# Reordered loads, two chunks of attention first, and out-stages held back until w3 @ w_out is there, in a retention-plus-FFN kernel on one core

## The chip, the core and the metric

The kernel runs on one core of one Trainium2 chip. The metric is the device time of one execution in microseconds. Times in the profile are microseconds from the first instruction, unless marked ns. PE is TensorE's matmuls, PEld its weight loads, DVE VectorE, ACT ScalarE, POOL GpSimd, SP the engine that issues the DMAs.

## The reference

q, k and v have 4 sequences, 8 heads, 768 positions and 64 values per head. A recurrent retention with a decay per head makes y, which is laid out as 3072 tokens of 512 values, and a multiplicative FFN follows:

```python
gamma = 1.0 - 2.0 ** (-5.0 - np.arange(H))
for t in range(S):
    state = gamma * state + einsum('bhd,bhe->bhde', k[:, :, t], v[:, :, t])
    y[:, :, t] = scale * einsum('bhd,bhde->bhe', q[:, :, t], state)
x = y.transpose(0, 2, 1, 3).reshape(B * S, H * D)      # 3072 x 512
h = ((x @ w1) * (x @ w2)) @ w3                         # w1, w2: 512 x 1024; w3: 1024 x 1024
out = h @ w_out                                        # w_out: 1024 x 512
```

## The kernel before

**Attention.** The tokens are cut into 24 chunks of 128, six to a sequence. For chunk n, `casts(n)` (line 181) makes fp16 copies of q on ScalarE and k on GpSimd, and GpSimd multiplies v by the decay table VS into one of three zero-padded buffers VP. `transposes(n)` (204) turns q and k on TensorE and evicts them: kT and qT on VectorE, the zero-padded QP in two halves on ScalarE. `scores(n)` (222) makes the masked score matrix `am`, `kv(n)` (240) the state for the next chunk (`s` on VectorE, `t` on GpSimd, tables GS), and `outputs(n)` (262) sums am against VP and the state against qT, and writes the chunk's part of XT with the table YS (271).

**FFN.** `ffn_tile` (276) takes a tile of 256 or 512 tokens. An A unit is four matmuls of a w1 column block against XT, evicted to `pa` by ScalarE; a B unit the same with w2, multiplied with pa by VectorE into `ht` (296). An out-stage (302) multiplies eight ht blocks by W3O = w3 @ w_out and writes 128 rows of the output. W3O is computed once: `w3_transpose` (151) and `w3_mm` (161), eight times each.

**Order of the work.** The schedule is manual: each engine runs its instructions in the order in which the program writes them, and waits where a semaphore says so. All DMAs are issued by SP, in program order too. The program writes: tables and zeroing (81 to 119), loads and casts of w_out and w3 (130 to 146) and the w3 product (171 to 175), then loads of chunks 0 and 1, loads and casts of w1 and w2 (360 to 368), more chunks, and the loop over 24 steps (373). Step n issues casts(n + 2), transposes(n + 1), scores(n), kv(n) and outputs(n), with FFN units pulled in between, spread evenly over the steps until the next tile is complete:

```python
m = -(-a // left)
parts = [m // 4 + (1 if i < m % 4 else 0) for i in range(4)]
```

The tiles are two of 256 tokens and five of 512; an out-stage of a tile follows each second pair of units of the next tile. Weights pass through six stage buffers (`wstage`), chunk loads through six buffers each for q, k and v, PSUM results of the FFN through three banks (`psF`).

Of the kernel before, what the change touches and what calls it, by code (L numbers as in the profile page):

```python
# [9 lines left out]
FP = mybir.dt.float32  # L10
HP = mybir.dt.float16
AF = mybir.ActivationFunctionType
MULT = mybir.AluOpType.mult
# [5 lines left out]
def kernel(  # L19
# [11 lines left out]
    nc = tc.nc  # L31
# [27 lines left out]
    def stage(w_ap, i, ncol):  # L59
        t = wstage.tile([128, ncol], FP, tag="wst", name="stg")  # L60
        nc.sync.dma_start(t[:, :], w_ap[i * 128 : (i + 1) * 128, :])
        return t
# [3 lines left out]
    def load_chunk(n):  # L66
        if n >= NSTEP:
            return
        b, c = divmod(n, NCH)
        tiles = []  # L70
        for nm, src in (("q", q), ("k", k), ("v", v)):
            t = ld.tile([128, 512], FP, tag=nm + "32", name=nm + "32")
            nc.sync.dma_start(
                t[:, :].rearrange("p (h d) -> p h d", d=D),
                src[b, :, c * C : (c + 1) * C, :].rearrange("h i d -> i h d"),
            )
            tiles.append(t)
        chunk_in[n] = tiles


    ident = const.tile([128, 128], FP, name="ident")
    make_identity(nc, ident[:, :])
    ident16 = const.tile([128, 128], HP, name="ident16")
    nc.vector.tensor_copy(ident16[:, :], ident[:, :])

# [5 lines left out]
    ip_f = const.tile([128, H], FP, name="ip_f")  # L91
    nc.vector.tensor_copy(ip_f[:, :], ip_i[:, :])
    if_f = const.tile([128, 128], FP, name="if_f")
    nc.vector.tensor_copy(if_f[:, :], if_i[:, :])


    VS = const.tile([128, H], FP, name="VS")
    YS = const.tile([128, NP, 128], FP, name="YS")
    GS = const.tile([128, NP, 128], FP, name="GS")
    nc.vector.memset(GS[:, :, :], 0.0)  # L100
    for h in range(H):
        lg = math.log(gam[h])
        p, r = h // 2, (h % 2) * 64
        nc.scalar.activation(VS[:, h : h + 1], ip_f[:, h : h + 1], AF.Exp, scale=-lg)
        nc.scalar.activation(YS[r : r + 64, p, :], if_f[r : r + 64, :], AF.Exp, scale=lg)
        nc.vector.memset(GS[r : r + 64, p, r : r + 64], gam[h] ** C)

    keep = const.tile([128, 128], FP, name="keep")
    nc.vector.memset(keep[:, :], 1.0)
# [6 lines left out]
    QP = [const.tile([128, NP, 2, 128], HP, name=f"qp{i}") for i in range(2)]  # L116
    VP = [const.tile([128, NP, 2, 128], HP, name=f"vp{i}") for i in range(3)]
    for t in QP + VP:
        nc.gpsimd.memset(t[:, :, :, :], 0.0)
# [4 lines left out]
    W1 = [wpool.tile([128, DFF], HP, name=f"w1_{i}") for i in range(4)]  # L124
    W2 = [wpool.tile([128, DFF], HP, name=f"w2_{i}") for i in range(4)]
    WO = [wpool.tile([128, DM], HP, name=f"wo_{i}") for i in range(8)]
    W3 = [wpool.tile([128, DFF], HP, name=f"w3_{i}") for i in range(8)]
    W3O = [wpool.tile([128, DM], HP, name=f"w3o_{i}") for i in range(8)]

    wo_st = [stage(moe_w_out, i, DM) for i in range(2)]  # L130
    w3_st = [stage(moe_w3, 0, DFF)]
    wo_st += [stage(moe_w_out, i, DM) for i in range(2, 4)]
    nc.scalar.copy(WO[0][:, :], wo_st[0][:, :])
    nc.scalar.copy(WO[1][:, :], wo_st[1][:, :])
    nc.vector.tensor_copy(W3[0][:, :], w3_st[0][:, :])  # L135
    nc.scalar.copy(WO[2][:, :], wo_st[2][:, :])
    nc.scalar.copy(WO[3][:, :], wo_st[3][:, :])
    for i in range(4, 8):
        t = stage(moe_w_out, i, DM)
        nc.scalar.copy(WO[i][:, :], t[:, :])  # L140
    for i in range(1, 8):
        t = stage(moe_w3, i, DFF)
        if i % 2 == 0:
            nc.vector.tensor_copy(W3[i][:, :], t[:, :])
        else:
            nc.scalar.copy(W3[i][:, :], t[:, :])


    w3t = {}

    def w3_transpose(f):
        ps = ps_t.tile([128, 1024], HP, tag="psT", name="psT")
        for g in range(8):
            nc.tensor.transpose(  # L154
                ps[:, g * 128 : (g + 1) * 128], W3[f][:, g * 128 : (g + 1) * 128], ident16[:, :]
            )
        t = att.tile([128, 1024], HP, tag="w3t", name="w3t")
        nc.vector.tensor_copy(t[:, :], ps[:, :])  # L158
        w3t[f] = t

    def w3_mm(f):
        t = w3t.pop(f)
        ps = ps_f.tile([128, DM], FP, tag="psF", name="psW")
        for g in range(8):
            nc.tensor.matmul(  # L165
                ps[:, :], lhsT=t[:, g * 128 : (g + 1) * 128], rhs=WO[g][:, :],
                start=(g == 0), stop=(g == 7),
            )
# [12 lines left out]
    def casts(n):  # L181
# [80 lines left out]
    def outputs(n):  # L262
# [10 lines left out]
        )  # L273


    def ffn_tile(tok0, TB):
        hts = []

        def unit(f):
            psA = ps_f.tile([128, TB], FP, tag="psF", name="psFA")  # L280
            for d in range(4):
                nc.tensor.matmul(  # L282
                    psA[:, :], lhsT=W1[d][:, f * 128 : (f + 1) * 128], rhs=XT[:, d, tok0 : tok0 + TB],
                    start=(d == 0), stop=(d == 3),
                )
            pa = fsb.tile([128, TB], FP, tag="pa", name="pa")
            nc.scalar.copy(pa[:, :], psA[:, :])  # L287
            yield
            psB = ps_f.tile([128, TB], FP, tag="psF", name="psFB")
            for d in range(4):  # L290
                nc.tensor.matmul(  # L291
                    psB[:, :], lhsT=W2[d][:, f * 128 : (f + 1) * 128], rhs=XT[:, d, tok0 : tok0 + TB],
                    start=(d == 0), stop=(d == 3),
                )
            ht = fsb.tile([128, TB], HP, tag=f"ht{f}", name=f"ht{f}")
            nc.vector.tensor_tensor(ht[:, :], pa[:, :], psB[:, :], MULT)  # L296
            hts.append(ht)
            yield

        def out_unit(tb):  # L300
            psO = ps_f.tile([128, DM], FP, tag="psF", name="psO")
            for f in range(8):
                nc.tensor.matmul(  # L303
                    psO[:, :], lhsT=hts[f][:, tb * 128 : (tb + 1) * 128], rhs=W3O[f][:, :],
# [4 lines left out]
            r0 = tok0 + tb * 128  # L309
            nc.sync.dma_start(out[r0 : r0 + 128, :], osb[:, :])  # L310

        return unit, out_unit, TB // 128

    tiles = [(0, 256), (256, 256)] + [(512 * i, 512) for i in range(1, 6)]

    def ffn_all():

        pending = []
        for tok0, TB in tiles:
            unit, out_unit, nout = ffn_tile(tok0, TB)  # L320
            for f in range(8):
                for _ in unit(f):
                    yield tok0 + TB
                if pending and f % 2 == 1:
                    fn, tb = pending.pop(0)
                    fn(tb)
                    yield tok0 + TB
            pending += [(out_unit, tb) for tb in range(nout)]
        while pending:
            fn, tb = pending.pop(0)  # L330
            fn(tb)
            yield 0

    need = []
    for i, (tok0, TB) in enumerate(tiles):
        nprev = tiles[i - 1][1] // 128 if i else 0
        need += [tok0 + TB] * (16 + nprev)
    need += [0] * 4
    gen = ffn_all()
    done = [0]  # L340

    def avail(ntok):

        m = done[0]
        while m < len(need) and need[m] <= ntok:
            m += 1
        return m - done[0]

    def pull(m):
        for _ in range(m):  # L350
            if done[0] < len(need):
                next(gen)
                done[0] += 1


    PRE = 5
    for n in range(2):
        load_chunk(n)
    w_st = []
    for nm, w_ap, dst in (("1", moe_w1, W1), ("2", moe_w2, W2)):  # L360
        for i in range(4):
            t = stage(w_ap, i, DFF)
            if i % 2 == 0:
                nc.vector.tensor_copy(dst[i][:, :], t[:, :])
            else:
                nc.scalar.copy(dst[i][:, :], t[:, :])
        if nm == "1":
            casts(0)
    for n in range(2, PRE):
        load_chunk(n)  # L370
    transposes(0)
    casts(1)
    for n in range(NSTEP):
        load_chunk(n + PRE)
        ready = n * C
        a = avail(ready)

        left = max(1, next((t0 + tb for t0, tb in tiles if t0 + tb > ready), NTOK) // C - n)
        m = -(-a // left)
        parts = [m // 4 + (1 if i < m % 4 else 0) for i in range(4)]  # L380
        casts(n + 2)
        transposes(n + 1)
        pull(parts[0])
        scores(n)
        pull(parts[1])
        t_new = kv(n)
        pull(parts[2])
        outputs(n)
        Tst[0] = t_new
        pull(parts[3])  # L390
    pull(len(need))
# [30 lines left out]
```

## Time and profile before

| | |
|---|---|
| median of 3 runs | 235.93 us (235.54 to 236.34) |
| profiled execution | 236.38 us |
| its span, first to last instruction | 234.7 us |
| TensorE matmuls busy | 194.7 us, 83% of the span |
| VectorE, ScalarE, GpSimd busy | 120.0, 105.5, 67.7 us |
| mean granted TensorE clock | 0.978 of full |
| DMA | 35.9 MB, mean 153 GB/s |

The profile has the busy time of each engine, 40 slices of the span, the chain of work that ended last followed back from the end, and groups of instructions by line with the mean time of one and what ended the idle time before them. Matmuls are pipelined, so the mean duration of one is longer than the distance between two. The profiled execution lies 0.45 us above the median of the runs.

### The profile page before, as it was taken

To read this page: it belongs to the slowest core of one execution; us is meant where nothing else is said; L and a number is where in the kernel's file an instruction comes from. 1 tells how busy PE (TensorE), PEld (TensorE's weight loads), DVE (VectorE), ACT (ScalarE), POOL (GpSimd) and SP (SyncE) were. 2 spreads that over 40 slices of the span, in tenths; PEclk is the share of its full clock that TensorE was granted. 3 is DMA by queue.
4 is the path that set the end of the run, shared out by engine and by line. 5 is a ranking of instruction groups with operands and counts; after the bars stand their busy time and mean duration, and the time that the engine had idled before them with its cause. 6 is when DMAs were issued, how large, how long until landed. Compare 5 with 4: busy or idle time off the path is not lost.

```text
span 234.7 us, 3859 instructions
## 1 busy us (share of the span) xinstructions
PE 194.7 (83%) x1408; PEld 116.2 (49%) x1408; DVE 120.0 (51%) x225; ACT 105.5 (45%) x193; POOL 67.7 (29%) x102
## 2 busy tenths in 40 slices
PE   0100899458988798999999999999999999999993
PEld 0100455237875585556655555555555555544441
DVE  3403224349776568667765576654666556432300
ACT  8443222774553454356435433554434542334332
POOL 4500330035545343424720553242332322000000
PEclk9999999857999999999999999999999999999999
DMA  5599994899997769586955566865601111011123
GB/s 196 196 355 375 210 376 172 254 213 219 211 216 148 170 142 188 129 182 146 218 84 144 118 124 157 179 144 123 136 1 47 45 45 47 27 64 45 47 89 135
DMA packets 81811, 35.91 MB, mean 153 GB/s; under 512 B 75648, under 2 KB 75648, under 8 KB 81792
## 3 DMA queue, kind: packets, MB, share of 16 engines
q1 hardware_dynamic: 81792, 35.66, 61.1%
q8 instruction: 11, 0.18, 0.4%
q14 instruction: 8, 0.07, 0.1%
HBM read 29.36 MB, written 6.29 MB: 152 GB/s over the span
## 4 chain that ended last, share of the span: by engine, by line
PE 63%; DVE 14%; ACT 8%; DMA 7%; issue 5%; SPq 1%; DVEq 0%; ACTq 0%
PE psO L303 18%; PE psFA L282 14%; PE psFB L291 10%; DVE am L232 8%; PE psW L165 7%; DMA stg<-in_moe_w_dram 5%; ACT qp L219 3%; PE psY L267 3%; ACT pa L287 2%; PE psA L229 2%; PE psT L210 2%; PE psT L212 2%; DMA stg<-in_moe_w_out_dram 2%; DVE ht L296 2%; PE psT L154 2%
## 5 line engine op out<-in xcount | busy, mean ns | idle before, releaser
L296 DVE TENSOR_TENSOR ht<-pa,psFB 128x512 f16<-128x512 f32 (+1 forms) x56 | 34.0, 607 | 51.6 <-ACT pa L287 33.3
L291 PE MATMUL psFB<-xt,w 128*128 128x512 f16 (+1 forms) x224 | 50.7, 349 | 2.6 <-ACT pa L287 2.5
L282 PE MATMUL psFA<-xt,w 128*128 128x512 f16 (+1 forms) x224 | 50.7, 349 | 0.9 <-DVE xt L271 0.9
L303 PE MATMUL psO<-w3o,ht 128*128 128x512 f16 x192 | 44.7, 380 | 0.0
L308 ACT ACTIVATE osb<-psO 128x512 f32<-128x512 f32 x24 | 14.3, 597 | 64.1 <-PE psO L303 64.1
L259 POOL TENSOR_TENSOR t<-s,GS 128x512 f16<-128x512 f32 x16 | 20.4, 1272 | 65.6 <-DVE s L258 57.1
L287 ACT COPY pa<-psFA 128x512 f32<-128x512 f32 (+1 forms) x56 | 28.8, 525 | 19.1 <-PE psFA L282 18.6
L196 POOL TENSOR_TENSOR vp<-v,VS 128x256 f16<-128x256 f32 x48 | 28.5, 615 | 13.6 <-PE psY L270 8.6
L232 DVE TENSOR_TENSOR am<-psA,keep 128x512 f16<-128x512 f32 x48 | 30.8, 682 | 0.4 <-PE psA L229 0.3
L291 PEld LDWEIGHTS <-w 128*128 128x128 f16 x224 | 21.3, 98 | 19.2 <-issue 3.3
L188 POOL CAST k<-k 128x512 f16<-128x512 f32 x24 | 14.6, 610 | 46.8 <-DMA k<-in_k_dram 36.7
L282 PEld LDWEIGHTS <-w 128*128 128x128 f16 x224 | 20.7, 98 | 13.8 <-DVE xt L271 0.8
L303 PEld LDWEIGHTS <-ht 128*128 128x128 f16 x192 | 18.1, 98 | 18.9
L154 PE MATMUL psT<-ident,w 128*128 128x128 f16 x64 | 5.7, 242 | 23.2 <-DVE w3t L158 13.7
L218 ACT COPY qp<-psT 64x512 f16<-64x512 f16 x24 | 13.9, 578 | 17.0 <-DVE qT L217 7.1
L267 PE MATMUL psY<-am,vp 128*128 128x128 f16 x96 | 18.0, 221 | 3.9 <-DVE am L232 2.1
L216 DVE COPY kT<-psT 128x512 f16<-128x512 f16 x24 | 10.2, 423 | 20.0 <-PE psT L212 19.9
L268 PE MATMUL psY<-am,vp 128*128 128x128 f16 x96 | 18.1, 223 | 0.0
L154 PEld LDWEIGHTS <-w 128*128 128x128 f16 x64 | 4.9, 109 | 25.0 <-DVE w L135 9.4
L271 DVE TENSOR_TENSOR xt<-psY,YS 128x512 f16<-128x512 f32 x24 | 16.4, 685 | 0.5 <-PE psY L270 0.3
L165 PE MATMUL psW<-wo,w3t 128*128 128x512 f16 x64 | 16.5, 409 | 0.0
L229 PE MATMUL psA<-qp,kT 128*128 128x256 f16 x96 | 15.3, 285 | 0.0
(49 smaller groups left out, 203.3 us busy)
## 6 DMA issues: line engine op xcount, KB each, us to landing
stg<-in_moe_w_dram SPq DMA_DIRECT2D x16, 512.0 KB, 6.7
q<-in_q_dram SPq DMA_DIRECT2D x24, 256.0 KB, 4.8
k<-in_k_dram SPq DMA_DIRECT2D x24, 256.0 KB, 4.9
v<-in_v_dram SPq DMA_DIRECT2D x24, 256.0 KB, 4.8
out_dram<-osb SPq DMA_DIRECT2D x24, 256.0 KB, 2.0
stg<-in_moe_w_out_dram SPq DMA_DIRECT2D x8, 256.0 KB, 3.9
```

The source lines that it names most:

```text
L165: nc.tensor.matmul(ps[:, :], lhsT=t[:, g * 128 : (g + 1) * 128], rhs=WO[g][:, :], start=(g == 0), stop=(g == 7),)
L196: nc.gpsimd.tensor_tensor(vp[:, :, r, r * 64 : r * 64 + 64], v32[:, :].rearrange("j (p s e) -> j p s e", s=2, e=64)[:, :, r, :], VS[:, :]. ...
L229: nc.tensor.matmul(ps[:, i, :, :], lhsT=kT[:, p, :], rhs=qp[:, p, :, :], start=True, stop=True)
L232: nc.vector.tensor_tensor(am[:, half * 2 : half * 2 + 2, :, :].rearrange("j p s i -> j (p s) i"), ps[:, :, :, :].rearrange("j p s i -> j ( ...
L259: nc.gpsimd.tensor_tensor(t16[:, :, :], s32[:, :, :], GS[:, :, :], MULT)
L267: nc.tensor.matmul(ps[:, p, :], lhsT=vp[:, p, 0, :], rhs=am[:, p, 0, :], start=True, stop=False)
L268: nc.tensor.matmul(ps[:, p, :], lhsT=vp[:, p, 1, :], rhs=am[:, p, 1, :], start=False, stop=(c == 0))
L282: nc.tensor.matmul(psA[:, :], lhsT=W1[d][:, f * 128 : (f + 1) * 128], rhs=XT[:, d, tok0 : tok0 + TB], start=(d == 0), stop=(d == 3),)
L287: nc.scalar.copy(pa[:, :], psA[:, :])
L291: nc.tensor.matmul(psB[:, :], lhsT=W2[d][:, f * 128 : (f + 1) * 128], rhs=XT[:, d, tok0 : tok0 + TB], start=(d == 0), stop=(d == 3),)
L296: nc.vector.tensor_tensor(ht[:, :], pa[:, :], psB[:, :], MULT)
L303: nc.tensor.matmul(psO[:, :], lhsT=hts[f][:, tb * 128 : (tb + 1) * 128], rhs=W3O[f][:, :], start=(f == 0), stop=(f == 7),)
```

## The change

**Loads.** SP issues chunks 0 and 1 first, then the left column halves of w1 and w2 (w1 and w2 of a row block side by side in one stage tile), chunks 2 and 3, the right halves, chunks 4 and 5, then w_out (four loads) and w3 (eight), then chunks 6 to 9. The stage buffers are still six, and a w3 tile has four fp16 buffers of its own (`w3h`) in place of eight lasting ones.

**Tables and zeroing.** QP and VP are zeroed by VectorE, as fp32 words; GpSimd writes the logarithms of the decay, and ScalarE makes VS in one exponential and YS in four.

**Order.** Chunks 0 and 1 go through attention before any FFN. Then units f = 0 to 3 of the first tile run between chunks 2 and 3, those of the second tile behind them, units 4 to 7 of both between chunks 4 and 5, and all units of the third tile with the casts of w_out and w3 between them. The w3 product follows, with the start of chunks 6 and 7 in its end. Only then do out-stages come: the six of the first three tiles head the queue from which steps 6 to 23 take their units, by estimated cost instead of by count. The tiles are five of 256 tokens, three of 512 and one of 256.

```diff
+    def load_w12(half):
+        got = []
+        for d in range(4):
+            t = new_stage()
+            for i, w in enumerate((moe_w1, moe_w2)):
+                dma_in(
+                    t[:, i * 512 : (i + 1) * 512],
+                    w[d * 128 : (d + 1) * 128, half * 512 : (half + 1) * 512],
+                )
+            got.append(t)
+        return got
...
+    load_chunk(0)
+    load_chunk(1)
...
+    def zero(t):
+        nc.vector.memset(t[:, :, :, :].rearrange("p a b c -> p (a b c)").bitcast(FP), 0.0)
...
-    for t in QP + VP:
-        nc.gpsimd.memset(t[:, :, :, :], 0.0)
...
+    def pull(self, cost, ntok):
+        self.credit += cost
+        while self.units and self.units[0][0] <= ntok and self.credit >= self.units[0][1] / 2:
+            need, c, fn = self.units.pop(0)
+            fn()
+            self.credit -= c
...
+    w12a = load_w12(0)
+    load_chunk(2)
+    load_chunk(3)
+    w12b = load_w12(1)
+    load_chunk(4)
+    load_chunk(5)
+
+    casts(0)
+    transposes(0)
+    casts(1)
+    scores(0)
+    transposes(1)
...
+    outputs(1, t_new)
+    cast_w12(0, w12a)
+    wo_st = load_wo()
+    w3_st = [load_w3(f) for f in range(8)]
...
+    for i in range(8):
+        fill.run(2)
+        if i < 2:
+            cast_wo(wo_st, i + 2)
+        elif i < 6:
+            cast_w3(w3_st, i - 2)
+    w3_transpose(0)
+    for f in range(8):
+        if f + 4 < 8:
+            cast_w3(w3_st, f + 4)
+        if f + 1 < 8:
+            w3_transpose(f + 1)
+        if f == 5:
+            casts(6)
+        if f == 7:
+            transposes(6)
+            casts(7)
+        w3_mm(f)
+
+    fill.units = f0.o_units() + f1.o_units() + f2.o_units()
```

The order of SP's queue at the start. Before (`stg` is a weight's stage tile; moe_w stands for w1, w2 and w3):

```order
L61 DMA stg<-in_moe_w_out_dram 128x512 x2
L61 DMA stg<-in_moe_w_dram 128x1024
L61 DMA stg<-in_moe_w_out_dram 128x512 x6
L61 DMA stg<-in_moe_w_dram 128x1024 x7
L73 DMA q_392<-in_q_dram 128x8x64
L73 DMA k_394<-in_k_dram 128x8x64
L73 DMA v_396<-in_v_dram 128x8x64
```

The same queue of the changed kernel:

```order
L60 DMA q_87<-in_q_dram 128x8x64
L60 DMA k_89<-in_k_dram 128x8x64
L60 DMA v_91<-in_v_dram 128x8x64
L60 DMA q_93<-in_q_dram 128x8x64
L60 DMA k_95<-in_k_dram 128x8x64
L60 DMA v_97<-in_v_dram 128x8x64
L60 DMA stg<-in_moe_w_dram 128x512 x8
L60 DMA q_189<-in_q_dram 128x8x64
```

Sixteen loads of w_out and w3 stood ahead of the first q; now six chunk loads stand ahead of the first weight, and w_out comes behind chunk 5.

VectorE's queue of the changed kernel, from the second transposed chunk to the first FFN product (`w_0`, `w_2` are fp16 tiles of w1 and w2 side by side, `s` the state before its decay):

```order
L248 COPY kT<-psT 128x512
L249 COPY qT<-psT 128x512
L287 TENSOR_TENSOR t_281<-psK,GS 128x512
L303 TENSOR_TENSOR xt<-psY,YS 128x4x128
L264 TENSOR_TENSOR am<-psA_294,keep 128x512
L264 TENSOR_TENSOR am<-psA_298,keep 128x512
L290 TENSOR_TENSOR s_308<-psK,t_281 128x512
L303 TENSOR_TENSOR xt<-psY,YS 128x4x128
L175 CAST w_0_161<-stg 128x1024
L175 CAST w_2_163<-stg 128x1024
L335 TENSOR_TENSOR ht_353<-pa,psF 128x256
```

The casts of w1 and w2, which stood ahead of all attention, now stand behind the second xt write and ahead of the first product.

ScalarE's queue of the changed kernel around the third tile, from the last units of the second (`wo` and `w3h` are fp16 tiles of w_out and w3):

```order
L331 COPY pa<-psF 128x256 x2
L177 CAST wo_165<-stg 128x1024
L177 CAST wo_166<-stg 128x1024
L331 COPY pa<-psF 128x256 x3
L177 CAST wo_167<-stg 128x1024
L331 COPY pa<-psF 128x256
L177 CAST wo_168<-stg 128x1024
L331 COPY pa<-psF 128x256 x2
L177 CAST w3h<-stg 128x1024
L331 COPY pa<-psF 128x256 x2
L177 CAST w3h<-stg 128x1024
```

The casts of w_out and w3 stood at the head of this queue; now they stand between the evictions of units.

## Rows read from the trace of the kernel before

**Rows 1.** The page: matmul busy time, and TensorE's share in 40 slices, in tenths.

```profile
PE 194.7 (83%) x1408; PEld 116.2 (49%) x1408; DVE 120.0 (51%) x225; ACT 105.5 (45%) x193; POOL 67.7 (29%) x102
...
PE   0100899458988798999999999999999999999993
```

**Rows 2.** The chain that ended last, in order of time: start, us, what.

```profile
15.55 7.29 DMA stg<-in_moe_w_dram
...
24.20 1.01 PE psT L154 x8
25.22 3.26 PE psW L165 x8
28.48 0.45 PE psT L154 x8
28.93 1.73 PE psW L165 x8
...
43.28 0.59 ACT w3o L169
...
45.76 0.53 ACT q L186
...
57.97 0.60 PE psFA L282 x4
58.56 0.44 PE psFB L291 x4
...
99.73 0.86 PE psFA L282 x4
...
122.51 1.73 PE psO L303 x8
...
144.42 1.73 PE psO L303 x8
...
222.44 8.65 PE psO L303 x40
231.15 0.60 ACT osb L308
```

**Rows 3.** Four stretches of time, with busy us of each engine.

```profile
core 0: us, PE busy (x) PEld busy (x) DVE busy (x) ACT busy (x) POOL busy (x), PEclk, DMA share, GB/s
2.00:4.00 2.00, 0.00 (x0) 0.00 (x0) 1.50 (x10) 1.94 (x11) 0.00 (x0) 1.00 0.84 299
16.00:18.00 2.00, 0.00 (x0) 0.11 (x1) 0.33 (x1) 1.04 (x1) 0.00 (x0) 1.00 1.04 424
50.00:55.00 5.00, 4.69 (x35) 3.99 (x36) 3.56 (x7) 2.37 (x5) 2.94 (x5) 0.50 1.14 220
56.00:58.00 2.00, 1.47 (x21) 1.22 (x21) 2.00 (x5) 1.31 (x3) 0.69 (x1) 1.00 1.24 221
```

**Rows 4.** The q loads: time from issue to landing over all 24.

```profile
DMA to landing us min/median/max: 3.3/4.8/7.4
```

**Rows 5.** VectorE's timeline: XT writes of chunks 1, 3 and 7; start, us.

```profile
57.22 0.69 DVE L271 TENSOR_TENSOR xt<-psY,YS 128x512 f16<-128x512 f32 x1
...
69.28 0.68 DVE L271 TENSOR_TENSOR xt<-psY,YS 128x512 f16<-128x512 f32 x1
...
91.55 0.68 DVE L271 TENSOR_TENSOR xt<-psY,YS 128x512 f16<-128x512 f32 x1
```

**Rows 6.** Groups by line and shape: count | busy us, mean ns | idle before.

```profile
L366 ACT CAST w<-stg 128x1024 f16<-128x1024 f32 x4 | 4.0, 1046 | 0.0
L119 POOL MEMSET vp<- 128x1024 f16 x3 | 2.7, 951 | 0.0
L364 DVE CAST w<-stg 128x1024 f16<-128x1024 f32 x4 | 2.6, 688 | 2.2 <-DMA stg<-in_moe_w_dram 2.2
L135 DVE CAST w<-stg 128x1024 f16<-128x1024 f32 x1 | 2.4, 2441 | 2.9 <-DMA stg<-in_moe_w_dram 2.9
```

More of the change, by code (lines that the diff above doesn't have):

```diff
@@ L56, with dma_in @@
     ctx.enter_context(tc.manual_schedule())
[L59 to L62, printed above, removed]
+    def dma_in(dst, src):
+        nc.sync.dma_start(dst, src)
     chunk_in = {}
@@ L113 @@
     )
-    QP = [const.tile([128, NP, 2, 128], HP, name=f"qp{i}") for i in range(2)]
-    VP = [const.tile([128, NP, 2, 128], HP, name=f"vp{i}") for i in range(3)]
-    for t in QP + VP:
-        nc.gpsimd.memset(t[:, :, :, :], 0.0)
+    VS = const.tile([128, H], FP, name="VS")
+    YS = const.tile([128, NP, 128], FP, name="YS")
+    GS = const.tile([128, NP, 128], FP, name="GS")
+    vs_x = const.tile([128, H], FP, name="vs_x")
+    nc.vector.tensor_tensor(vs_x[:, :], ip_i[:, :], LGH[:, :], MULT)
@@ new lines @@
+    if_f = const.tile([128, 128], FP, name="if_f")
+    nc.vector.tensor_copy(if_f[:, :], if_i[:, :])
+    nc.scalar.activation(VS[:, :], vs_x[:, :], AF.Exp)
+    for p in range(NP):
+        nc.scalar.activation(YS[:, p, :], if_f[:, :], AF.Exp, scale=LGP[:, p : p + 1])
+    zero(QP[0])
+    zero(VP[0])
+    zero(QP[1])
+    zero(VP[1])
+    nc.vector.memset(GS[:, :, :], 0.0)
+    for h in range(H):
+        p, r = h // 2, (h % 2) * 64
+        nc.vector.memset(GS[r : r + 64, p, r : r + 64], gam[h] ** C)
@@ L121 @@
+    zero(VP[2])
     XT = xpool.tile([128, NP, NTOK], HP, name="xt")
[L124 to L127, printed above, removed]
+    W12 = [wpool.tile([128, 2, 2, 512], HP, name=f"w12_{i}") for i in range(4)]
+    WO = [wpool.tile([128, 2, DM], HP, name=f"wo_{i}") for i in range(4)]
@@ L128 @@
     W3O = [wpool.tile([128, DM], HP, name=f"w3o_{i}") for i in range(8)]
[L130 to L144, printed above, removed]
-        else:
-            nc.scalar.copy(W3[i][:, :], t[:, :])
-    w3t = {}
+    W3h = {}
+    w3t = {}
+    def cast_to(dst, src, on_dve):
+        if on_dve:
+            nc.vector.tensor_copy(dst, src)
+        else:
+            nc.scalar.copy(dst, src)
+    def cast_w12(half, got):
+        for d in range(4):
+            cast_to(W12[d][:, half, :, :].rearrange("p a n -> p (a n)"), got[d][:, :], d % 2 == 0)
@@ L308, in out_unit @@
             nc.scalar.activation(osb[:, :], psO[:, :], AF.Copy, scale=final_scale)
-            r0 = tok0 + tb * 128
+            r0 = self.tok0 + tb * 128
             nc.sync.dma_start(out[r0 : r0 + 128, :], osb[:, :])
[L312 to L370, printed above, removed]
+        def ab_units(self, fs):
+            cost = self.TB / 512 * 0.87
+            need = self.tok0 + self.TB
+            u = []
+            for f in fs:
+                u.append((need, cost, lambda f=f: self.a_unit(f)))
+                u.append((need, cost, lambda f=f: self.b_unit(f)))
+            return u
@@ new lines, in o_units, with __init__, available, run @@
+        def o_units(self):
+            return [(0, 1.73, lambda tb=tb: self.o_unit(tb)) for tb in range(self.TB // 128)]
+    class Queue:
+        def __init__(self):
+            self.units, self.credit = [], 0.0
+        def available(self, ntok):
+            s = 0.0
+            for need, cost, _ in self.units:
+                if need > ntok:
+                    break
+                s += cost
+            return s
+        def pull(self, cost, ntok):
[4 more added lines that the diff above has]
+                self.credit -= c
+            if not self.units or self.units[0][0] > ntok:
+                self.credit = 0.0
+        def run(self, m=None):
+            for _ in range(len(self.units) if m is None else m):
+                self.units.pop(0)[2]()
@@ new lines, with step @@
+    fill = Queue()
+    def step(n, look=1):
+        ready = n * C
+        nxt = next((t0 + tb for t0, tb in tiles if t0 + tb > ready), NTOK)
+        share = fill.available(ready) / max(1, nxt // C - n)
+        casts(n + 1 + look)
+        transposes(n + 1)
+        fill.pull(share * 0.25, ready)
+        scores(n)
+        fill.pull(share * 0.25, ready)
+        t_new = kv(n)
+        fill.pull(share * 0.25, ready)
+        outputs(n, t_new)
+        fill.pull(share * 0.25, ready)
+    tiles = [(256 * i, 256) for i in range(5)] + [(1280 + 512 * i, 512) for i in range(3)] + [(2816, 256)]
@@ L371 @@
+    w12a = load_w12(0)
[5 more added lines that the diff above has]
+    casts(0)
     transposes(0)
     casts(1)
[L373 to L390, printed above, removed]
@@ L391 @@
-    pull(len(need))
+    scores(0)
+    transposes(1)
+    t_new = kv(0)
+    outputs(0, t_new)
+    scores(1)
+    t_new = kv(1)
+    outputs(1, t_new)
+    cast_w12(0, w12a)
+    wo_st = load_wo()
+    w3_st = [load_w3(f) for f in range(8)]
+    f0 = Ffn(*tiles[0], 4)
+    fill.units = f0.ab_units(range(0, 4))
+    fill.run(2)
+    casts(2)
+    transposes(2)
+    fill.run(2)
+    scores(2)
+    casts(3)
+    fill.run(1)
+    t_new = kv(2)
+    fill.run(1)
+    transposes(3)
+    outputs(2, t_new)
@@ new lines @@
+    fill.run(2)
+    scores(3)
+    t_new = kv(3)
+    outputs(3, t_new)
+    f1 = Ffn(*tiles[1], 4)
+    fill.units = f1.ab_units(range(0, 4))
+    fill.run(4)
+    cast_w12(1, w12b)
+    fill.run(4)
+    fill.units = f0.ab_units(range(4, 8)) + f1.ab_units(range(4, 8))
+    fill.run(2)
+    casts(4)
+    transposes(4)
+    fill.run(2)
+    scores(4)
+    fill.run(2)
+    casts(5)
+    t_new = kv(4)
+    fill.run(2)
+    transposes(5)
+    outputs(4, t_new)
+    fill.run(2)
+    scores(5)
+    fill.run(2)
@@ new lines @@
+    cast_wo(wo_st, 0)
+    cast_wo(wo_st, 1)
+    t_new = kv(5)
+    fill.run(2)
+    outputs(5, t_new)
+    fill.run(2)
+    f2 = Ffn(*tiles[2], 4)
+    fill.units = f2.ab_units(range(8))
+    for n in range(6, 10):
+        load_chunk(n)
+    for i in range(8):
+        fill.run(2)
+        if i < 2:
[14 more added lines that the diff above has]
+        w3_mm(f)
@@ new lines @@
+    fill.units = f0.o_units() + f1.o_units() + f2.o_units()
+    late = []
+    for i, (tok0, TB) in list(enumerate(tiles))[3:]:
+        f = Ffn(tok0, TB, 4 if TB == 256 else 2)
+        for j in range(0, 8, 2):
+            fill.units += f.ab_units((j, j + 1))
+            if late:
+                fill.units.append(late.pop(0))
+        fill.units += late
+        late = f.o_units()
+    fill.units += late
+    for n in range(6, NSTEP):
+        load_chunk(n + 4)
+        step(n)
+    fill.run()
```

109 lines of the change are left out of this document (59 added, 50 removed).

## The prediction

> **What bounds the kernel now.** I read the page's busy times first, then the chain of waits, then stretches of time, and last groups by shape. TensorE is busy 83% of the span, and its slices show where the rest lies: next to nothing in the first four slices of 5.9 us, a dip in the eighth and ninth, and nines from the seventeenth on [rows 1]. So from about 98 us the kernel is bound by TensorE, and what can be won lies ahead of that.
>
> The chain says what fills the start [rows 2]. The weights w_out and w3 come in until 22.8 us, the product w3 @ w_out begins in earnest with the transposes at 24.20 and its last eviction starts at 43.28, and only at 45.76 does the first q chunk get its cast, though attention needs nothing of these weights. The first FFN matmul issues at 57.97. The last out-stage matmul ends at 222.44 + 8.65 = 231.1 us, and 3.6 us of eviction and store follow, up to 234.7.
>
> The clock matters too. Between 50 and 55 us the granted clock is 0.50 with TensorE busy 4.69 of 5 us, and at 56 to 58 it is 1.00 [rows 3]: levels of 1.2 and 2.4 GHz. The chain shows the same levels at the start of w3: the first eight w3 matmuls take 3.26 us, the next eight 1.73.
>
> **Prices.** At the full clock, from rows 2: eight transposes 0.45 us, so 0.056 each; a unit of four 256-column matmuls 0.44, one of 512 columns 0.86; an out-stage or w3 group of eight 1.73. A chunk's attention is 24 matmuls of 128 columns and four of 256: 24 x 0.056 + 0.44 = 1.78 us. A step in the dense part lasts (144.42 - 122.51) / 3 = 7.30 us for four units, one out-stage and one chunk, 6.95 us of work: 0.35 lost per step.
>
> **The change, step by step.**
>
> *Chunk 0 first.* Its q DMA now goes out at about 0.8 us, where the first DMA goes out today. A q load takes 3.3 us to land at the least, 4.8 in the median, 7.4 at most [rows 4], so the cast starts between 4.1 and 8.2 us. I take 5.3, near the median, since the queue is empty then, and because ScalarE has its exponentials to do first (five instead of sixteen). That is 40.5 us before 45.76.
>
> *Two chunks before any FFN.* From that cast to the end of the second xt write takes 57.22 + 0.69 - 45.76 = 12.1 us today [rows 2, 5]. scores(0) now stands ahead of the second transposes, which frees it of one q cast of 0.62; I take 11.6 us, so xt(1) ends at 16.9.
>
> *w1/w2 casts behind it.* VectorE's two casts are queued behind xt(1), so the first unit waits for both: 2 x 0.69 = 1.4 us by the casts of today's w1, w2; ScalarE's two (1.05 each) are done earlier [rows 6]. The one w3 cast made while GpSimd zeroed took 2.44, so the upper bound is 4.9. I take 1.4, because GpSimd's zeroing, beside which the long one ran, is gone, but keep the bound: GpSimd is now making t and the next k at that moment. FFN starts at 16.9 + 1.4 = 18.3; say 18.4.
> The Trainium skill, "SBUF — State Buffer", section "Who interferes with whom", says that a VectorE cast in a two-port mode and a GpSimd instruction exclude each other for a whole instruction. It agrees with 2.44 beside 0.69, and speaks against this placing: by it the pair would end near the upper bound, and the whole some 2 to 3 us later.
>
> *Zeroing.* Five memsets of 0.95 us leave GpSimd [rows 6] for VectorE, which has nothing to do before the first transposes. Both lie beside the wait for chunk 0: nothing. If chunk 0 landed at 4.1 they would show, by under 1 us.
>
> *Work from 18.4 on.* FFN: 48 units of 512 columns, 41.3; 96 of 256, 42.2; 24 out-stages, 41.5. Attention of 22 chunks: 39.2, less 0.22 for each of three first and four last chunks of a sequence, 1.5. The w3 product, moved from the start to behind f2: 8 x (0.45 + 1.73) = 17.4. Together 180.1 us.
>
> *Cold clock.* TensorE does little before 18.4, so I expect 1.2 GHz there and, for a first stretch like that of 50 to 55, the low level still: half of 5 us lost, 2.5. Bounds: 0, and the second rival.
>
> *Idle TensorE from 18.4 on.* Today the stretch from 57.97 to 231.1, 173.1 us, holds 124.4 of FFN and 37.2 of attention, so 11.5 idle. Now:
> - chunks 2 and 3: xt(1) to xt(3) took 12.1 us with 16 units [rows 5]; only eight are ready now (half of w1, w2 is there). Work 3.5 + 3.6 + 2.5 cold = 9.6. The chain from transposes over evictions to xt does not shorten, so I take 12.4: 2.8 idle.
> - chunks 4 and 5: filled as today's chunks 2 and 3, 0.4 each: 0.8.
> - ScalarE's weight casts: two pairs of 1.05 stand in its queue between evictions of units (after the first four f1 units; before kv(5)). TensorE runs three psF banks ahead, about 1.3 us: 0.8 each. Six casts in f2: 0.5. Start of w3: 0.7. Sum 2.8.
> - steps 6 to 23: 18 x 0.35 = 6.3, and 0.6 more in steps 10 to 13, which have only 2.6 us of units each. Steps of that kind took (91.55 - 69.28) / 4 = 5.57 us today for 4.95 of work [rows 5]. Sum 8.7.
>
> Together 15.1. The DMA queue holds no term. In it w_out and w3 wait for stage buffers, thus for casts ScalarE makes at some 43 to 50 us, and chunk 6 waits behind w3. But w3 lands 2 to 3 us after each cast and is needed one every 2.17, and chunk 6 is needed near 67: covered. If the casts slip, the w3 loop is late next.
>
> **Sum.** 18.4 + 180.1 + 2.5 + 15.1 = 216.1 for the last matmul, + 3.6 = 219.7, against the span of 234.7: 15.0 less. The profiled execution took 236.38, 0.45 over the median 235.93. From the median: **220.9 us**.
>
> **Rivals.**
> *Loads late (0.17).* Chunk loads run at 220 GB/s [rows 3]; 4 KB-row weights at 424; the first 2 KB-row weights at 299. I reckoned w1, w2 near 300 to 400. If everything ran at 220, the first half of w1 and w2 (14 loads of 262 KB) would land at about 2 + 16.7 = 18.7 instead of some 16, and chunk 5 (34 loads) at 42.5, where I need it near 36. That makes FFN start 1.5 late and chunk 5 another 4: 226. For it: in 50 to 55 the engines are full at that rate. Against: the weights are 4 of 8.9 MB.
>
> *The clock stays down (0.04), ending slower.* The work from 18.4 to the w3 loop is 48 units and four chunks, 28.2 us at the full clock. If the waits for chunks 2 to 5 kept TensorE at 1.2 GHz throughout, it would cost 28.2 rather than 2.5: 247. It decides from the point where 17.5 us of this work ran at half. For it: 0.50 was held at a busy share of 0.94 from 50 to 55. Against: it rose right after, and then never fell, also in slices with 7 and 8 tenths [rows 1, 3].
>
> *The start overlaps better (0.15).* Cast at 4.1, no cold loss, and idle time as today's 11.5: 220.9 - 1.2 - 2.5 - 3.6 = 213.6.
>
> *The change does nothing for the end (0.02).* If w3 took TensorE's time at its new place and the steps behind were starved, 236. The printed order speaks against it: six tiles' worth of units lie behind it.
>
> **How the numbers follow.** The forecast has 0.62. The range is 213.5 to 228.0: it takes in the good rival, the loads' rival, and the two casts at 4.9 with the late landing of chunk 0. About 2 in 10 lie outside, beyond these ends and in the slow rival. Under and over 0.3% is what a measurement here can tell from no change; all but the second and the last rival are well below it: faster 0.94, same 0.02, slower 0.04.
>
> **What would show it.** First q cast near 5 us; first FFN matmul near 18; xt(3) near 30; the w3 loop from about 55 to 73 without waits longer than 0.3; then steps like today's, with TensorE nines to the end; granted clock 0.5 until 22 to 25 and 1.0 after. Wrong if w1/w2 casts wait for DMA, if the clock falls again in the waits for chunk 3, or if ScalarE's queue starves the w3 loop.

## The result and the profile after

| | before | changed |
|---|---|---|
| median of 4 runs | 235.74 us | 222.94 us (222.27 to 223.81) |
| profiled execution | 236.38 us | 223.81 us |
| its span | 234.7 us | 222.1 us |

The ratio is 0.9465, with a 95% interval of 0.9408 to 0.9521: 12.8 us less by the medians. Ratios are of means, and a run more than 1.5% above the fastest of its kernel is left out of them. The forecast was 220.9, within 213.5 to 228.0, so the time came out 2.0 us over it. Several terms were wrong, and two large errors cancelled.

The page of the changed kernel, the lines of [rows 1] and the granted clock:

```profile
PE 194.0 (87%) x1536; PEld 128.3 (58%) x1536; DVE 125.0 (56%) x244; ACT 104.0 (47%) x194; POOL 65.1 (29%) x114
...
PE   0366769688999989988999999999999999999992
...
PEclk9997976999999999999999999999999999999999
```

TensorE works from the second slice on, but has holes until the tenth, where [rows 1] had almost nothing in four slices and a dip in two. The granted clock dips in the fourth slice and falls again in the sixth and seventh.

The chain that ended last, as in [rows 2] (start, us, what):

```profile
10.87 5.84 DMA q<-in_q_dram
16.75 1.91 DVE w L175 x2
18.70 0.41 PE psF L318 x2
...
31.03 0.70 DVE xt L303
31.78 6.16 PE psF L318 x32
...
49.20 0.96 ACT wo L177
50.16 0.91 issue
51.07 0.38 ACT pa L331
51.48 0.42 DVE ht L335
51.90 0.61 DVE xt L303
...
61.53 0.61 PE psT L196 x8
62.14 1.73 PE psW L207 x8
...
161.48 1.73 PE psO L340 x8
168.44 1.73 PE psO L340 x8
...
212.89 5.20 PE psO L340 x24
218.16 0.60 ACT osb L345
```

The first unit waits for VectorE's weight casts until 18.7. The profile puts a q load ahead of these casts, but they do not read it: in VectorE's queue they stand behind xt(1), which ends at 16.83. XT of chunk 3 is written at 31.03, and the 32 matmuls behind it take 6.16 us where 3.5 are due at the full clock. At 49 a ScalarE cast of w_out stands ahead of an eviction, and through VectorE's product ahead of XT of chunk 5. The w3 product starts at 61.5, some 6 us later than forecast. From 126 us on the chain is TensorE alone, and a step takes 168.44 - 161.48 = 6.96 us: the work itself, 6.95.

Stretches of time, columns as in [rows 3]:

```profile
18.10:31.78 13.68, 9.76 (x89) 7.61 (x89) 8.44 (x17) 4.84 (x10) 5.83 (x8) 0.81 1.09 264
31.78:61.50 29.72, 25.32 (x220) 20.40 (x220) 16.59 (x37) 17.59 (x34) 5.42 (x8) 0.91 0.78 235
61.50:80.70 19.20, 18.14 (x137) 10.30 (x137) 6.78 (x11) 8.90 (x15) 5.39 (x9) 1.00 1.04 213
80.70:126.00 45.30, 42.50 (x407) 32.15 (x405) 31.07 (x64) 24.19 (x49) 18.77 (x27) 1.00 0.84 172
126.00:180.00 54.00, 54.00 (x405) 31.61 (x403) 37.04 (x65) 27.32 (x48) 21.02 (x30) 1.00 0.56 120
...
30.00:36.00 6.00, 5.11 (x29) 3.54 (x26) 2.39 (x6) 1.84 (x4) 3.06 (x4) 0.51 1.22 221
```

Set against the work that each stretch holds by the forecast's own prices, the changed kernel loses 6.6 us from 18.1 to 31.8 (7.1 of work), 8.8 until 61.5 (20.9), 1.3 until 80.7, and 3.1 from there to the last matmul at 218.1. The tail behind it is 4.0 us, for a forecast of 3.6.

**Two outcomes of one kernel.** The four runs had mean granted clocks of 0.975, 0.974, 0.997 and 1.000, and took 223.81, 223.57, 222.30 and 222.27 us. So the same program has two outcomes, 1.4 us apart. Only the slower one has a profile of this kernel, and in it the clock falls twice, to 0.50 from 20 to 22 us and again from 30 to 36; a mean of 1.000 leaves room for neither fall. The 1.4 us is therefore the worth of the whole outcome, and not of the fall at 30 alone.

### The profile page after: what moved, and what is told of

It reads as the page before. It is cut to its first block, busy times and chain, and to the rows that moved or that the text cites. A ratio compares the mean times of both kernels' runs of the same rounds, so it can differ in the third digit from the quotient of the medians.

```text
span 222.1 us, 4183 instructions
## 1 busy us (share of the span) xinstructions
PE 194.0 (87%) x1536; PEld 128.3 (58%) x1536; DVE 125.0 (56%) x244; ACT 104.0 (47%) x194; POOL 65.1 (29%) x114
## 4 chain that ended last, share of the span: by engine, by line
PE 77%; ACT 7%; SPq 4%; issue 4%; DVE 4%; DMA 3%; ACTq 0%; DVEq 0%
PE psF L318 35%; PE psO L340 19%; PE psW L207 5%; SPq L60 4%; PE psA L261 4%; DMA q<-in_q_dram 3%; PE psT L242 3%; PE psT L244 2%; ACT qp L251 2%; PE psY L299 2%; PE psY L300 2%; PE psY L302 2%; PE psK L282 2%; PE psT L196 1%; ACT pa L331 1%
## 5 line engine op out<-in xcount | busy, mean ns | idle before, releaser
L318 PE MATMUL psF<-xt,w 128*128 128x256 f16 (+1 forms) x576 | 99.1, 316 | 6.5 <-ACT pa L331 3.0
L318 PEld LDWEIGHTS <-w 128*128 128x128 f16 x576 | 56.1, 101 | 30.7 <-issue 5.7
L335 DVE TENSOR_TENSOR ht<-pa,psF 128x256 f16<-128x256 f32 (+1 forms) x72 | 36.5, 508 | 44.7 <-ACT pa L331 19.9
L331 ACT COPY pa<-psF 128x256 f32<-128x256 f32 (+1 forms) x72 | 31.3, 444 | 33.5 <-PE psF L318 32.4
L299 PE MATMUL psY<-am,vp 128*128 128x128 f16 x96 | 17.4, 224 | 1.4 <-DVE am L264 1.0
L300 PE MATMUL psY<-am,vp 128*128 128x128 f16 x96 | 17.4, 225 | 0.0
L261 PEld LDWEIGHTS <-kT 128*128 128x128 f16 x96 | 9.5, 100 | 12.8 <-issue 7.1
L242 PE MATMUL psT<-ident,q 128*128 128x128 f16 x96 | 10.0, 230 | 7.3 <-ACT q L222 7.3
L207 PE MATMUL psW<-wo,w3t 128*128 128x512 f16 x64 | 15.1, 379 | 0.0
L222 ACT CAST q<-q 128x512 f16<-128x512 f32 x24 | 14.8, 618 | 0.0
L302 PE MATMUL psY<-qT,t 128*128 128x128 f16 x80 | 14.8, 221 | 0.0
```

Of the source, the lines that this page charges most:

```text
L207: nc.tensor.matmul(ps[:, :], lhsT=t[:, g * 128 : (g + 1) * 128], rhs=WO[g // 2][:, g % 2, :], start=(g == 0), stop=(g == 7),)
L261: nc.tensor.matmul(ps[:, i, :, :], lhsT=kT[:, p, :], rhs=qp[:, p, :, :], start=True, stop=True)
L299: nc.tensor.matmul(ps[:, p, :], lhsT=vp[:, p, 0, :], rhs=am[:, p, 0, :], start=True, stop=False)
L300: nc.tensor.matmul(ps[:, p, :], lhsT=vp[:, p, 1, :], rhs=am[:, p, 1, :], start=False, stop=(c == 0))
L302: nc.tensor.matmul(ps[:, p, :], lhsT=Tst[0][:, p, :], rhs=qT[:, p, :], start=False, stop=True)
L318: nc.tensor.matmul(ps[:, :], lhsT=W12[d][:, half, which, col : col + 128], rhs=XT[:, d, self.tok0 : self.tok0 + self.TB], start=(d == 0), ...
```

## The experiments

Eleven kernels ran besides the changed one. Unless another kernel is named, times are medians set against a second measurement of the changed kernel, which gave 223.73 us, all four executions with a clock of 0.975 to 0.976. Ratios are to the kernel before on the same chip. The kernels on load order, on the third tile's place and on QP first were timed in another group than this second measurement, and before took 236.46 us there against 235.79 here; by the ratios, the three slower ones lie 0.4 to 0.7 us less far behind, and QP first 0.6 further ahead.

> The changed kernel itself, beside the others of this group: about 222.9 us, as measured already; the experiments of this group are read against this run.

223.73 us, ratio 0.9498 (0.9445 to 0.9552).

### What the load order is worth

**Weights ahead of chunks 0 and 1.**

```diff
+    w12a = load_w12(0)
     load_chunk(0)
     load_chunk(1)
...
-    w12a = load_w12(0)
     load_chunk(2)
     load_chunk(3)
```

> The changed kernel with the left halves of w1 and w2 loaded ahead of chunks 0 and 1. Theory (the chain from chunk 0 sets the start): the first q cast comes about 5.2 us later, near 9.8, the FFN starts near 23, and the end is 4 to 5 us later. Rival (FFN needs both, so the order of the two does not matter): within 1.5 us.

228.69 us, ratio 0.9681 (0.9611 to 0.9752): 5.0 us slower. The theory holds, the size of its first step does not. ScalarE's first q cast, then TensorE's first unit, in this kernel's timeline:

```profile
11.95 0.62 ACT L223 CAST q<-q 128x512 f16<-128x512 f32 x1 [7.30 <-DMA q<-in_q_dram]
...
24.96 0.60 PE L319 MATMUL psF<-xt,w 128*128 128x256 f16 x2 [1.65 <-DVE w L176]
```

The cast is 7.4 us later than with chunks first (4.57), the FFN 6.9, the end 5.0. All four runs had clocks of 0.998 to 0.999; against the changed kernel's runs at that clock (222.3) the end is 6.4 later, so nearly all of the late start stays to the end.

**Both halves of w1 and w2 ahead of chunks 2 and 3.**

```diff
-            t = new_stage()
+            if half == 1 and d == 2:
...
     w12a = load_w12(0)
+    w12b = load_w12(1)
     load_chunk(2)
     load_chunk(3)
-    w12b = load_w12(1)
```

> The changed kernel with the loads of the right halves of w1 and w2 moved ahead of chunks 2 and 3 (their last two stage tiles lie in a buffer that is free until later). Theory (the loads of chunks 2 and 3 are just in time): 2 MB at some 380 to 400 GB/s make them 5.5 us later, XT of chunk 3 about 4 us later, and the end 3 to 5 us later. Rival (the chain over evictions sets the stretch to XT of chunk 3, not the loads): within 1 us.

226.52 us, ratio 0.9593 (0.9536 to 0.9649): 2.8 us slower, the theory's way and a little under its 3 to 5. GpSimd's k casts of chunks 2 and 3 wait for their loads:

```profile
23.91 0.61 POOL L227 CAST k<-k 128x512 f16<-128x512 f32 x1 [6.22 <-DMA k<-in_k_dram]
...
27.62 0.61 POOL L227 CAST k<-k 128x512 f16<-128x512 f32 x1 [1.30 <-DMA k<-in_k_dram]
```

XT of chunk 3 came at 35.88 instead of 31.05. So the column halves pay because they let chunks 2 and 3 in sooner. Two of the four runs had a clock of 0.997 to 0.998 and took no less (226.19 and 226.51); against the changed kernel's runs at such a clock, the loss is 4.1.

### What zeroing off GpSimd is worth

**Back on GpSimd in the changed kernel.**

```diff
     def zero(t):
-        nc.vector.memset(t[:, :, :, :].rearrange("p a b c -> p (a b c)").bitcast(FP), 0.0)
+        nc.gpsimd.memset(t[:, :, :, :], 0.0)
```

> The changed kernel with the five zeroing memsets back on GpSimd. Theory (the start is one chain from chunk 0 to the second XT write): five memsets of 0.95 us hold GpSimd until about 8.5 us, so the first k cast, at 5.34 in the changed kernel, starts about 3.2 later, and kT of chunk 0, which now waits for VectorE's last memset until 7.87, about 1.9 later; FFN starts 1.9 later and the end moves with it: 1.5 to 2 us slower. Rival (the start is set by the loads of w1 and w2, whose last ScalarE cast ends at 17.9): no change, within 0.5 us.

225.94 us, ratio 0.9580 (0.9519 to 0.9641): 2.2 us slower, a little over the theory. The one run at a clock of 0.998 took 224.58, 2.3 over the changed kernel's at such a clock. GpSimd's timeline of this kernel:

```profile
6.42 1.85 POOL L119 MEMSET vp<- 128x1024 f16 x2
8.21 0.61 POOL L224 CAST k<-k 128x512 f16<-128x512 f32 x1
```

The k cast of chunk 0 starts at 8.21 instead of 5.34, FFN at 19.87 instead of 18.11. The start is one chain from chunk 0 on; the loads of w1 and w2 do not set it. They are not far behind: in the changed kernel ScalarE's last cast, which waits for its load, ends at 17.86, and VectorE's at 18.65.

**On VectorE in the kernel before, alone.** The same edit, the other way, without the rest of the change.

> The kernel before, with one part of the change alone: QP and VP zeroed by VectorE. Theory (the first w3 cast lasts 2.44 us because GpSimd's memsets run beside it, and SP's next loads wait 2.4 us for that cast): the cast takes 0.69, the loads of w3 come 1.75 us earlier, and the end does too. Rival (the loads wait next for w_out's casts on ScalarE, or the clock takes it back): the cast is shorter, the end within 0.5 us of before.

233.49 us (10 runs) against 235.75 (19 runs), ratio 0.9908 (0.9873 to 0.9943): 2.3 us faster. The cast that took 2441 ns in [rows 6]:

```profile
L135 DVE CAST w<-stg 128x1024 f16<-128x1024 f32 x1 | 0.7, 694 | 0.7 <-DMA stg<-in_moe_w_dram 0.7
```

Nothing but the engine of the memsets was changed, so the 2.44 us was GpSimd's doing, as the rule of the Trainium skill that the prediction names ("SBUF — State Buffer", "Who interferes with whom") has it. The loads behind the cast come sooner, and the first w3 matmul issues at 22.23 instead of 25.22 [rows 2]: 3.0 us sooner, of which 2.3 reach the end.

### The waits in the start

**TensorE kept busy at the wait for chunk 3.** 24 matmuls whose result nobody reads are added.

```diff
+    def keep_busy(m):
+        ps = ps_f.tile([128, 256], FP, tag="psF", name="psD")
+        for _ in range(m):
+            nc.tensor.matmul(ps[:, :], lhsT=ident16[:, :], rhs=XT[:, 0, 0:256], start=True, stop=True)
...
     fill.run(2)
+    keep_busy(10)
     scores(3)
     t_new = kv(3)
+    keep_busy(6)
     outputs(3, t_new)
+    keep_busy(8)
```

> The changed kernel with 24 extra matmuls of 256 columns whose result nobody reads, placed on TensorE where it waits for chunk 3 (ten before scores(3), six before outputs(3), eight behind it). Theory (the granted clock falls to 0.50 at 30 us after that wait, and the units from 31.78 pay for it): the clock stays at 1.00, the 32 matmuls that took 6.16 us take 3.5, and the end comes 1.5 to 2.7 us earlier. Rival (what those units lose is waited for again behind them, at chunk 4): no gain, or up to 0.5 us slower by the added matmuls.

222.27 us (221.57 to 222.30), ratio 0.9429 (0.9373 to 0.9484): 1.5 us faster, at the lower end of the theory. From 30 to 36 us, where the changed kernel's last row above has a clock of 0.51:

```profile
30.00:36.00 6.00, 5.03 (x49) 4.23 (x48) 4.34 (x8) 2.95 (x6) 3.50 (x4) 1.00 1.03 205
```

It is also exactly what the changed kernel does by itself in its better outcome (222.27, 222.30). And the profiles part before any added matmul, the first of which issues at 27.20. The scores of chunk 1, four matmuls of 256 columns, in the changed kernel and then in this one:

```profile
13.85 0.60 PE L261 MATMUL psA<-qp,kT 128*128 128x256 f16 x4 [0.82 <-DVE xt L303]
13.86 1.01 PE L261 MATMUL psA<-qp,kT 128*128 128x256 f16 x4 [0.82 <-DVE xt L303]
```

In the changed kernel's profile TensorE is at its full pace here, and the clock falls at 20 and at 30 us. In this one it is still near half of it, comes to full pace at about 22 us, and the clock does not fall from there to 36. (The granted clock is given as 1.00 for both at 13.85, so only the durations tell the two apart.) The next kernel has no added matmuls; it too takes 1.01 us for these scores, and keeps a clock of 1.00 from 18 to 52 us. So no gain of the added matmuls is shown: the better outcome alone is worth the 1.4 to 1.5 us. Why an execution takes the one or the other is open.

**The third tile's units behind the w3 product.**

```diff
-    fill.units = f2.ab_units(range(8))
...
-        fill.run(2)
         if i < 2:
...
-    fill.units = f0.o_units() + f1.o_units() + f2.o_units()
+    fill.units = f0.o_units() + f1.o_units() + f2.ab_units(range(8)) + f2.o_units()
```

> The changed kernel with the third tile's sixteen units moved from before the w3 product to behind it (into the queue of steps 6 to 9), so that only casts stand between chunk 5 and w3. Theory (the units between are only a filler, and TensorE lacks work later, in steps 8 to 13): the w3 product starts about 8 us earlier, near 54, its loads keep up, and the end comes 1 to 2 us earlier. Rival (the loads of w3 wait for stage buffers and need the 7 us of these units as cover): the w3 loop gets waits of 1 us and more, and the end is 2 to 5 us later.

225.86 us, ratio 0.9572 (0.9512 to 0.9633): 2.1 us slower, and 3.6 over the changed kernel's better outcome (222.3), whose clock it comes near (0.989 to 0.997). The rival's time, partly by another way: the waits, of 1.4 and 0.8 us, stand at the start of the w3 product and not between its groups. From this kernel's chain, columns as in [rows 2]:

```profile
47.66 1.04 ACT wo L177
48.72 3.25 DMA stg<-in_moe_w_dram
52.00 0.69 DVE w3h L175
52.69 0.63 DVE w3t L200
53.36 1.01 PE psT L196 x8
54.37 2.82 PE psW L207 x8
57.19 0.58 PE psT L196 x8
57.77 1.73 PE psW L207 x8
...
74.19 1.73 PE psO L340 x8
```

The product's first matmuls come at 54.37, where the changed kernel has them at 62.14: 7.8 us sooner. But from 50.6 to 53.4 TensorE had run only eight transposes (0.62 us), since this load of w3 waited for a stage buffer, and so for ScalarE's cast of w_out at 47.66. The first group then takes 2.82 us instead of 1.73, at a granted clock of 0.63 from 52 to 56. The first out-stage comes at 74.19, against 80.72: 6.5 sooner, with 16 units of 0.44, 7.0 us, still to do. That leaves it 0.5 behind. Another 1.5 is lost later, most of it in this stretch, columns as in [rows 3]:

```profile
80.00:90.00 10.00, 8.79 (x80) 6.93 (x78) 5.60 (x12) 4.85 (x11) 1.80 (x3) 1.00 0.60 143
```

TensorE has no such gap from 80 to 90 in the kernel with the added matmuls (busy all 10 us). So the 7 us of units are no mere filler: ahead of the product they cover the wait for w3, and behind it they meet a new wait on ScalarE's evictions.

**w_out cast on GpSimd.**

```diff
     def cast_wo(got, i):
-        cast_to(WO[i][:, :, :].rearrange("p a n -> p (a n)"), got[i][:, :], False)
+        nc.gpsimd.tensor_copy(WO[i][:, :, :].rearrange("p a n -> p (a n)"), got[i][:, :])
```

> The changed kernel with the four casts of w_out on GpSimd instead of ScalarE. Theory (ScalarE's queue holds up units, products and XT of chunk 5 between 49 and 55 us): 1 to 2 us faster. Rival (another wait takes the place, or GpSimd's casts hold the loads of w3 longer): within 0.5 us, or up to 1 us slower.

222.40 us, ratio 0.9421 (0.9350 to 0.9492): 1.3 us faster, as the theory says. XT of chunk 5 came at 50.79 instead of 51.68, the w3 product at 60.52 instead of 61.85. The clock was 0.977 in three of four runs, so this gain is not that of the clock; the fourth, at 1.000, took 221.00, again 1.3 under the changed kernel's at that clock.

**QP evicted first.**

```diff
-        nc.vector.tensor_copy(kT[:, :, :], ps[:, 1, :, :])
-        nc.vector.tensor_copy(qT[:, :, :], ps[:, 0, :, :])
         nc.scalar.copy(qp[0:64, :, 0, :], ps[0:64, 0, :, :])
         nc.scalar.copy(qp[64:128, :, 1, :], ps[64:128, 0, :, :])
+        nc.vector.tensor_copy(kT[:, :, :], ps[:, 1, :, :])
+        nc.vector.tensor_copy(qT[:, :, :], ps[:, 0, :, :])
```

> The changed kernel with the order of evictions after the transposes reversed: ScalarE's two copies into QP first, then kT and qT on VectorE (the two engines read the same PSUM tile one after the other in either order). Theory (in the stretch to 52 us scores wait for the chain kT, qT, QP, QP of 2.0 us): the chain to scores is QP, QP, kT, 1.6 us, 0.4 less for each of the waiting chunks, and the end comes 1 to 2 us earlier. Rival (VectorE now waits behind ScalarE's evictions and casts): no gain, or up to 2 us slower.

221.38 us, ratio 0.9374 (0.9318 to 0.9430): 2.3 us faster at clocks of 0.976 to 0.984, a little over the theory's 2. XT of chunk 3 came at 29.23 instead of 31.05, of chunk 5 at 47.17 instead of 51.68; the gain is made in the start. The 1.8 us to chunk 3 is the chain's. From there on the clock has a part in it: this profile has the fall at 20 us but not the one at 30. The end does not depend on that alone, since the run with the lowest mean clock, 0.976, took 221.42.

**The same in the kernel before.**

> The kernel before with QP evicted first. Theory (the chain to scores is waited for only in the stretch where attention has little beside it, up to chunk 8, about 0.4 us a chunk): 1.5 to 3 us faster than before, as in the changed kernel. Rival (there TensorE's queue is the bound and the order of evictions is hidden): within 0.7 us.

236.44 us, ratio 1.0006 (0.9966 to 1.0047): nothing, as the rival has it, but not for its reason. Attention comes later and not sooner: XT of chunk 0 at 55.40 instead of 53.90, of chunk 1 at 60.34 instead of 57.22 [rows 5], of chunk 8 at 100.46 instead of 98.12. VectorE's kT of chunk 1 and the masking of chunk 0's scores (`am`) behind it, before and then here:

```profile
51.20 0.42 DVE L216 COPY kT<-psT 128x512 f16<-128x512 f16 x1 [3.04 <-PE psT L212]
51.88 1.28 DVE L232 TENSOR_TENSOR am<-psA,keep 128x512 f16<-128x512 f32 x2
...
52.77 0.42 DVE L218 COPY kT<-psT 128x512 f16<-128x512 f16 x1 [2.47 <-PE psK L250]
53.44 1.28 DVE L232 TENSOR_TENSOR am<-psA,keep 128x512 f16<-128x512 f32 x2
```

In this kernel kT starts only when ScalarE's two copies are done, at 52.7, and since the next chunk's kT stands ahead of `am` in VectorE's queue, `am` is 1.6 us later. In the changed kernel the scores of each of the first six chunks are written ahead of the next chunk's transposes, so this wait is not there. The clock also rose later; the stretch from 55 to 58 us is still at 0.50, where [rows 3] has 1.00 from 56 on:

```profile
55.00:58.00 3.00, 2.49 (x20) 2.06 (x18) 1.56 (x4) 1.72 (x3) 1.19 (x2) 0.50 1.29 219
```

Its table of VectorE's waits from 46 to 100 us (total us, times, longest us) has one long entry:

```profile
DVE kT L218 <- ACT qp L217: 16.9, 9, 4.3
```

The longest, 4.3 us, is that of chunk 0, whose copies stand behind two casts of w1 and w2 in ScalarE's queue. What is lost in the start is made up later: from 98 to 195 us TensorE is busy for 96.7 us, against 95.3 before. That the order of the queues alone makes the difference between the two kernels was read from the traces and not tried.

**QP first and w_out on GpSimd; then the added matmuls too.**

> The changed kernel with QP evicted first and w_out cast on GpSimd, which alone gave about 2.3 and 1.3 us. Theory (two separate waits, chunk by chunk and behind chunk 5): they add, to about 220.0 us. Rival (one stretch to the w3 loop, in which a new wait takes the place, such as the loads of w3): no better than the better of the two, 221.4.

220.70 us (219.88 to 221.34), ratio 0.9357 (0.9283 to 0.9431): between the two theories. Two runs at a clock of 0.984 took 219.88 and 220.12, two at 0.974 took 221.34 and 221.28.

> As the last, with the 24 extra matmuls at the wait for chunk 3. Theory (they make the better of two outcomes of the clock certain): the better times of the last run, all of them at a mean clock near 1.0, about 0.7 us under its median. Rival (with QP first the wait is too short for the clock to fall): the same or up to 0.7 us slower.

219.68 us (219.51 to 220.32), ratio 0.9310 (0.9250 to 0.9369): the fastest kernel here, 16.1 us under before and 4.1 under the changed kernel. It is 1.0 under the last, where the theory had 0.7, but the clocks (0.981 to 0.996) are mixed, and the intervals of the two overlap. The profiles again part before the first added matmul at 25.88: from 16 to 24 us the clock is 1.00 here and 0.57 in the last kernel. What the matmuls give is not settled.

## Why the prediction was right, and where its terms were not

**First cast.** Forecast 5.3, measured 4.55: inside 4.1 to 8.2, near its early end.

**The chain of two chunks.** Forecast 11.6 us, measured 16.14 + 0.69 - 4.55 = 12.28. A cause that the trace shows is VectorE's row of memsets: kT of chunk 0 starts at 7.87, though its transposes issue at 6.0 and take 0.6, since the memsets of the GS table (from 5.49) and the last zeroing memset (from 7.47) stand ahead of it. xt(1) ends at 16.83 (forecast 16.9): the cast came 0.75 early and the chain took 0.7 longer, and that they cancel so closely is luck.

**The casts behind it.** Forecast 1.4 us for the two, measured 1.9. The row the forecast took (688 ns) held for the second; the first took 1.30, beside this GpSimd instruction:

```profile
16.23 1.27 POOL L291 TENSOR_TENSOR t<-s,GS 128x512 f16<-128x512 f32 x1 [4.88 <-DVE s L290]
...
16.75 1.90 DVE L175 CAST w<-stg 128x1024 f16<-128x1024 f32 x2
```

The bound of 4.9 was far off: the 2.44 came beside a row of memsets, and here one instruction was in the way. The rule that the prediction names from the Trainium skill is borne out in kind, but a price taken from it has to count what GpSimd has queued at that moment. FFN started at 18.10, for 18.4.

**Zeroing at nothing: the step that failed most clearly.** On VectorE the memsets do not hide fully: kT of chunk 0 waits 1.3 us for the row in which they stand, the case of an early chunk 0, which the text put at under 1 us. And the same paragraph should have asked what they cost on GpSimd, where they stood: 2.2 us in the changed kernel and 2.3 in the one before. The sum was not hurt, since its anchor assumed k casts that find GpSimd free; the reading was. [rows 6] showed the 2.44 us cast beside them, and the text used it as a bound alone.

**Idle and cold from 18.4 on.** Forecast 15.1 + 2.5 = 17.6, measured 19.8 in the profiled execution, which is one of the slower outcome. By stretch:
- to xt(3): forecast 5.3, measured 6.6. Right in kind; the chain over evictions set it, as the run with QP first shows.
- from there to the w3 product: forecast 3.6 with the start of w3, measured 8.8. This is the term that was mis-sized most. 2.7 of it is the second fall of the clock (6.16 for 3.5 in the chain), which the text named only among what would make it wrong. At the end the whole slower outcome, both falls of the clock together, is worth 1.4. The w_out casts were put at up to 1.3 (0.8 and a part of 0.5), and taking them off ScalarE gave 1.3. The scores of chunks 4 and 5 wait 2.2 us for the second copy of QP, put at 0.8. The remaining 2.6, against 1.5 in the forecast, is spread over q casts, evictions and the start of the product, and was not tried apart.
- the w3 loop: no term but its work, measured 1.3, at the hand-over to the out-stages.
- steps 6 to 23: forecast 8.7, measured 3.1. The 0.35 us per step of today's dense part was carried over and is gone: from 126 to 180 us TensorE is busy for all 54. In the chain of before, VectorE's two am products stand in almost every step; now none does from 154 to 200. The new queue, which spreads units by cost, puts more of them between scores and outputs. That was read from the two traces and not tried apart.

**Loads late** (0.17): partly. Chunk rates were as feared, 217 to 225 GB/s from 2 to 8 us, but the units and chains before chunks 4 and 5 were later still, so the loads did not set them. **Clock stays down**: not throughout, but the second fall is a piece of it. **Better overlap**: not in the changed kernel, and even the fastest kernel here, at 219.7, is 6 us above its 213.6.

What the parts are worth, each undone alone, against the second measurement of the changed kernel: first chunks ahead of the weights 5.0, halves 2.8, zeroing 2.2, third tile ahead of w3 2.1. They add up to 12.1, but that is no proof that they are the 12.8. All four runs of that measurement are of the slower outcome; against the changed kernel's better one, runs at a like clock lose 6.4, 4.1, 2.3 and 3.6, which add up to more than the gain, so parts share waits. And some parts were not undone alone: that w3 stands behind two chunks of attention, the new tiles, the out-stages held back, and the queue that goes by cost, under which the steps lose 5.6 us less than forecast.

## What to carry to other kernels

When work is moved from one engine to another, price it where it stood as well as where it goes; a cover that hides the new place says nothing of what the old one cost. A stretch that is bound by a chain over several engines is shortened by the order of small evictions and casts in their queues, and the same edit gives nothing where the copy that now waits stands ahead of other work in its own engine's queue. Before a filler is moved, ask which load it covers where it stands, and what the clock does in the gap that it leaves. Before a gain of 1 to 2 us is put down to an edit, look for the first instruction at which the two profiles part: if it lies ahead of the edit, something else has made a part of the gain.

## What the runs showed of the hardware

The same program had two outcomes: 222.3 us at a mean granted clock of 1.00 and 223.7 at 0.975, in four executions two of each. In five profiles of kernels that are the same program up to 27 us (the changed kernel twice, w_out on GpSimd, the added matmuls, the third tile behind), they part at 13.85 us. Where four matmuls of 256 columns took 0.60 us there, the granted clock fell to 0.50 at 20 and again at 30 us; where they took 1.01, TensorE came to full pace at about 22 us and the clock stayed at 1.00 past 36. What was slower at 14 us was faster in the end. A comparison of such kernels by a difference of 1 to 2 us has to look at the clock of every run.

A VectorE cast of 0.69 us took 2.44 with three GpSimd memsets queued beside it, 1.30 with one GpSimd product under way, and 0.69 again when the memsets were moved.
